# A linear-attention and Fourier-mixing kernel on one core, with its opening stage rebuilt

## The chip, the core and the metric

The kernel runs on 1 core of one Trainium2 chip. The time is device microseconds of one execution, from the launch to the last output, as the median of several runs. Before the change it is 1011.36 us (3 runs, 1010.89 to 1011.57). The five engines of the core work through instruction queues of their own: TensorE (PE in the profile, its weight loads PEld), VectorE (DVE), ScalarE (ACT), GpSimd (POOL) and SyncE (SP). SP here only issues transfers, which run on 16 DMA engines.

## The reference

All of it is float32, with batch 8, 8 heads, 576 tokens, 64 columns to a head, and so 512 columns in all.

```python
def _attn_ref(q, k, v):                      # q, k, v: (8, 8, 576, 64)
    q_s = exp(q - max(q, -1)); q_s = q_s / (sum(q_s, -1) + 1e-9)
    k_s = exp(k - max(k, 2));  k_s = k_s / (sum(k_s, 2) + 1e-9)
    kv = einsum('bhsd,bhse->bhde', k_s, v)
    return einsum('bhsd,bhde->bhse', q_s, kv)

def _moe_ref(x, w_ch1, w_ch2):               # x: (8, 576, 512)
    mixed = real(fft(fft(x, axis=1), axis=2))
    u = x + mixed
    un = (u - mean(u, -1)) / sqrt(var(u, -1) + 1e-6)
    return u + maximum(un @ w_ch1, 0) @ w_ch2  # w: 512 x 2048, 2048 x 512
```

The kernel gets k transposed (columns by tokens), q and v with the heads side by side, and the two weight matrices as pairs of 32-bit words that it has to turn into float32 on the chip. Two tables come from the host: `ft` with cosines and sines over tokens, `cd` over columns.

## The kernel before

The work goes by groups of 512 tokens. Of a batch's 576 tokens, 512 make its own four tiles of 128 x 512; the 64 that are left are gathered from all batches into a ninth group. For each group come attention, folds of tokens and columns (which use the symmetry of the Fourier transform to quarter its products), two stages of products with `ft` and `cd`, a norm, and two layers of products with the weights. The first layer ("plain", lines 1435 to 1475) is computed directly for batch 0, while the weights are converted and combined; all later groups run on combined weights. No loop is on the chip: the program lists every step with a due time, sorts the steps, and so fixes the order of each engine's instructions. An engine never takes a later instruction first; where one waits, all behind it on that engine wait. The due times give an order and no clock.

The opening is written out by hand: the string `OPENING` names each step with its time. Steps `k00` to `k03` are batch 0's keys for pairs of heads (`max`, `exp`, four transposes `turn`, a copy `four`, and the product with the values `kv`); `k0 last` and `k0 fifth` transpose the last 128 tokens. A, B, C and D are batch 0's own tiles of queries and `t` the 128 rows of tokens that are shared with batch 1. They are exponentiated, transposed and multiplied by the key-value products, which stand as full 128 x 128 blocks in `kv0` (zeros off the two heads' blocks); a further product with `ones` gives the sums for the division. Then `tokens`, `columns`, `by` and `again` fold the rows on VectorE, `b0` to `b4` are the blocks of frequencies on TensorE (lines 1196 and 1199), `m0` and `m1` the second transform of the two halves of tokens (lines 1270, 1273), `s` the statistics of the four tiles, `normal`, `turn` and `laid` the normalized, transposed tiles. Among these stand `k10` to `k13`, the keys of batch 1 in the same way as batch 0's, and `c0`, the conversion of the first block of weights. `WARM` adds products whose result nobody reads.

The loads of the opening are issued by SP in the order that `loads_first` gives: keys of batch 0 (4 loads), the first half of the queries, the first half of the values (2), the second half of the queries, the shared tokens (4 loads of 32 rows, line 305), the other half of the values (2), 4 rows that replace rows of the shared tokens (line 308), the tables, keys and values of batch 1 (12), and eleven blocks of raw weights.

The first layer multiplies sixteen blocks of channels, `up(f)`, each of four products of 128 x 512 (line 1441). Block 0 runs as two halves of 256 columns (`half`, line 1450), since the tiles with c = 0 are normalized first. Each block of weights is converted by ACT (lines 409, 410), VectorE (403, 406) and POOL (411). VectorE also forms the combined weights (461) while the layer runs.

Later batches take their keys in another form, `keys(b)`: loads `kb` and `vt` with another layout (lines 676, 688), maxima on VectorE (732), an exchange between partitions, sixteen exponentials on ACT (736), transposes on VectorE (745), and products that use half of TensorE's columns (754).

Of the kernel before, what the change touches and what calls it, by code (L numbers as in the profile page):

```python
# [87 lines left out]
WARM = (3, 3), (24.7, 6), (41.9, 2), (43.45, 1), (44.5, 1)  # L88
# [4 lines left out]
10.80 A exp, 11.20 k00 kv, 11.30 k03 four, 11.84 B exp, 11.85 A turn, 12.20 C max, 12.30 k01 kv, 12.45 A copy,  # L93
12.80 D max, 12.95 B turn, 12.95 C less, 13.40 A ones, 13.55 B copy, 13.99 D less, 14.10 C exp, 14.20 k02 kv,
14.35 A inverse, 14.85 C turn, 15.00 t max, 15.14 D exp, 15.30 k03 kv, 15.75 t less, 15.95 D turn,
16.35 k0 scale0, 16.40 B ones, 16.47 t exp, 16.80 k0 scale1, 17.14 t inverse, 17.25 B kv, 17.99 B inverse,
18.22 A kv, 18.35 C copy, 18.39 t normal, 19.01 B out, 19.19 t turn, 19.32 D copy, 19.63 k10 max, 19.69 C ones,
19.84 t copy, 20.30 A out, 20.43 k10 exp, 20.49 C kv, 20.92 C inverse, 21.39 t fold, 21.46 D ones,
22.26 D kv, 22.40 C out, 22.51 D inverse, 23.53 D out, 23.60 t join, 23.65 k10 turn, 23.70 t kv, 24.15 tokens0,
24.36 t parts, 24.77 tokens1, 25.39 columns0, 25.46 k10 four, 25.75 columns1, 25.80 t rest, 26.23 by1, 26.59 by0,  # L100
26.80 c0 hi, 26.95 t folds, 27.45 c0 lo, 27.60 t rows, 27.70 again0, 28.00 again1, 28.50 tokens3, 28.60 b0 times,
29.12 tokens2, 29.58 b1 times, 29.74 columns3, 29.80 b0 copies, 30.10 columns2, 30.56 b4 times, 30.58 by2,
30.78 b1 copies, 30.94 by3, 31.42 again2, 31.72 again3, 31.76 b4 copies, 32.22 k12 max, 32.32 b2 times,
32.89 c0 shift, 33.02 k12 exp, 33.30 b3 times, 33.59 c0 sign, 33.78 b2 copies, 34.19 k13 max, 34.28 k12 turn,
34.31 c0 add, 34.50 b3 copies, 34.86 k11 max, 35.05 k13 exp, 35.20 m0 times, 35.81 k12 four, 36.10 k13 turn,
36.31 m0 copy, 36.55 m1 times, 36.66 k11 exp, 36.81 m0 sums, 37.42 k13 four, 37.61 k1 last, 37.71 m0 add0,
37.92 m1 copy, 38.07 k11 turn, 38.27 k1 fifth, 38.39 m0 add1, 38.42 m1 sums, 38.77 k11 four, 38.92 k10 kv,
39.22 s00, 39.27 roots, 39.67 k11 kv, 39.69 m1 add1, 39.97 s01, 40.42 k12 kv, 40.87 root0, 40.99 m1 add0,
41.17 k13 kv, 41.67 scales0, 41.87 s11, 42.02 normal01, 42.62 s10, 42.77 turn01, 43.37 normal00, 43.52 root1,
43.87 scales1, 43.89 normal11, 43.95 laid01, 44.02 turn00, 44.22 normal10, 44.77 laid00, 44.87 turn10,  # L110
45.47 turn11, 45.62 laid10, 46.22 laid11, 53.00 k1 inverse, 53.30 k1 scale0, 53.60 k1 scale1"""
# [30 lines left out]
class _Block:  # L142
    def __init__(self, ctx, tc, q, kT, v, w1, w2, ft, cd, out):
# [6 lines left out]
        self.ps = pool("ps", space=bass.MemoryType.PSUM)  # L150
        for n in ("ba", "bb", "bc"):
            self.ps.tile([P, 512], F32, tag=n, name=n)
        self.banks(0)
        ctx.callback(lambda: self.small_banks.__exit__(None, None, None))
# [7 lines left out]
        for b in range(2):  # L162
            t = c.tile([P, NR, DH + 1], F32, name=f"pairs{b}")
            nc.gpsimd.memset(t[:], 1.0)
            self.pairs.append(t)
        t = self.work.tile([P, KT, HD], F32, tag="Z", name="Z", bufs=1)
        self.kv0 = t[:].rearrange("p k n -> p (k n)")[:, 0:NR * P].rearrange("p (r n) -> p r n", r=NR)
        nc.gpsimd.memset(self.kv0, 0.0)

# [19 lines left out]

        self.ones = c.tile([P, NR, H], F32, name="ones")  # L190
        nc.gpsimd.memset(self.ones[:], 0.0)
        for h in range(2):
            nc.gpsimd.memset(self.ones[64 * h:64 * h + 64].rearrange("p r h -> p (r h)")[:, h::H + 2], 1.0)
# [39 lines left out]
    def banks(self, late):  # L233

        if late:
            self.small_banks.__exit__(None, None, None)
        self.late = late
        self.small_banks = self.tc.tile_pool(name=f"banks{late}", bufs=1, space=bass.MemoryType.PSUM)
        self.ps2 = self.small_banks.__enter__()

    def acc(self, shape, two=False):
        if self.late:
            t = self.two()[:, 0, :] if two else self.ps2.tile([P, 512], F32, tag="one", name="one")
        else:
            t = self.ps2.tile([P, 512], F32, tag="acc", name="acc", bufs=3)
        return t[:shape[0], :shape[1]]

    def two(self):
        return self.ps2.tile([P, 2, 512], F32, tag="two", name="two", bufs=2)

    def turned(self):
        if self.late:
# [17 lines left out]
    def warm(self, n):  # L270

        t = self.ps.tile([P, 512], F32, tag="ba", name="ba")
        for _ in range(n):
            self.nc.tensor.matmul(t[:, 0:2 * P], lhsT=self.ident[:], rhs=self.pairs[1][:].rearrange("p r n -> p (r n)")[:, 0:2 * P],
                                  start=True, stop=True)
# [4 lines left out]
    def loads_first(self, fetch):  # L280
# [9 lines left out]
        ks = [place(S) for _ in range(NR)]  # L290
        v = place(NC * D).rearrange("p (c n) -> p c n", n=D)
        own = [place(2 * D).rearrange("p (c n) -> p c n", n=D) for _ in range(2)]
        tail = place(D)

        at = NF * D - NR * (S + NC * P)
        k1, v1 = [place(S) for _ in range(NR)], [place(NC * P) for _ in range(NR)]
        self.second_at = k1, [t.rearrange("p (c n) -> p c n", n=P) for t in v1]
# [3 lines left out]
        def shared():  # L301
            flat = self.q[b:b + 2].rearrange("b s n -> (b s) n")
            for i in range(4):
                a = i * S // 2 + P
                load(tail[i * Q:(i + 1) * Q], flat[a:a + Q])

        def shared_firsts():
            load(tail[0:P:Q], self.q[b:b + 2].rearrange("b s n -> (b s) n")[::S // 2])
# [17 lines left out]
        def second(r):  # L326
            cols = slice(r * P, (r + 1) * P)
            t = self.second_at[1][r]
            load(self.second_at[0][r], self.kT[1, cols, :])
            load(t[:, 0:4, :], self.v[1, 0:512, cols].rearrange("(c p) n -> p c n", p=P))  # L330
            load(t[:, 4, :], self.v[1, S - P:, cols])
# [4 lines left out]
        return [(i / 100, step) for i, step in enumerate(order)]  # L336

# [18 lines left out]
    def tables(self):  # L356
        self.nc.sync.dma_start(self.ft[:], self.ft_dram)
        self.nc.sync.dma_start(self.cd[:], self.cd_dram)

    def weights(self):
# [23 lines left out]
        def convert(i):  # L386
# [5 lines left out]
            n = ("bc", "bb", "bc")[i] if i < 3 else "acc"  # L392
            if i < 26:
                t = self.ps.tile([P, 512], F32, tag=n, name=n)[:] if i < 3 else self.acc((P, D))
            else:

                t = hi.bitcast(F32)
# [114 lines left out]
    def attention_timed(self, b, start, end):  # L512
# [14 lines left out]
        for t, *some in visits:  # L527
            jobs = [self.t_times_kv(b) if it == "t" else self.own_times_kv(it, i == 1) for i, it in enumerate(some)]
# [23 lines left out]
    def first_keys(self, b):  # L552

        nc, V = self.nc, self.nc.vector
        ks, v = self.at_start[:2] if b == 0 else self.second_at
        v = [v[:, :, r * P:(r + 1) * P] for r in range(NR)] if b == 0 else v
        copy, box, top = nc.vector.tensor_copy if b == 0 else nc.scalar.copy, {}, {}
# [33 lines left out]
        def times(r):  # L591
            if r == 0:
                box["kv"] = self.acc((P, D)).rearrange("p (r n) -> p r n", n=P)
            for c in range(NC):
                left = self.kss[r][:, c, :] if c < 4 else self.fifth[:, r, :]
                nc.tensor.matmul(box["kv"][:, r, :], lhsT=left, rhs=v[r][:, c, :], start=c == 0, stop=c == NC - 1)

        def scale(h):
            s = slice(64 * h, 64 * h + 64)
            V.tensor_tensor(out=self.pairs[b][s, :, 0:DH] if b else self.kv0[s, :, s], in0=box["kv"][s, :, s],  # L600
                            in1=rec[s].unsqueeze(2).to_broadcast([64, NR, 64]), op=ALU.mult)
# [6 lines left out]
        for h in range(2):  # L608
            step(f"k{b} scale{h}", scale, h)
        return steps  # L610

    def opening(self, fetch, converted):
# [4 lines left out]
        steps = {**self.first_keys(0), **self.first_keys(1)}  # L617
# [16 lines left out]
        named("t kv,t parts,t folds,t rest,t rows", self.t_times_kv(0))  # L634
        for n, it in own.items():
            named(f"{n} max,{n} less,{n} exp", self.q_exp_spread(it))
            named(f"{n} turn,{n} copy", self.q_turn(it))
            named(f"{n} ones,{n} kv,{n} inverse,{n} out", self.q_times_kv(it))
        for name, f in zip(("tokens", "columns", "by", "again"), self.folded(0)):
            for i in range(4):  # L640
# [1334 lines left out]
```

## Time and profile before

| what | us |
|---|---|
| median of 3 runs, in all | 1011.36 |
| the profiled execution, in all | 1013.53 |
| its span, first to last instruction | 1011.7 |
| TensorE busy in the span | 999.8 |
| VectorE, ScalarE, GpSimd busy | 717.4, 493.9, 443.2 |
| first product of the first layer starts at | 50.78 |
| moved by DMA | 236.18 MB |

The profile takes one execution. Lines such as L1441 are lines of the kernel. "x8" counts records; a float32 product of TensorE leaves two records. A row of the stages ("11.03:27.73 ...") has the length, then each engine's busy time with its number of records, the granted share of TensorE's clock, the mean busy share of the 16 DMA engines, and GB/s. A row of a timeline has start, length, engine, line and operation, output and input, and in brackets the idle time before it and what ended that. A row of the groups by line ends with busy us, mean ns of one, and idle time before. The chain of waits is followed back from the last instruction; its rows have start, length, and what that time went to.

### The profile page before, as it was taken

To read this page: it belongs to the slowest core of one execution; us is meant where nothing else is said; L and a number is where in the kernel's file an instruction comes from. 1 tells how busy PE (TensorE), PEld (TensorE's weight loads), DVE (VectorE), ACT (ScalarE), POOL (GpSimd) and SP (SyncE) were. 2 spreads that over 40 slices of the span, in tenths; PEclk is the share of its full clock that TensorE was granted. 3 is DMA by queue.
4 is the path that set the end of the run, shared out by engine and by line. 5 is a ranking of instruction groups with operands and counts; after the bars stand their busy time and mean duration, and the time that the engine had idled before them with its cause. 6 is when DMAs were issued, how large, how long until landed. Compare 5 with 4: busy or idle time off the path is not lost.

```text
span 1011.7 us, 19333 instructions
## 1 busy us (share of the span) xinstructions
PE 999.8 (99%) x7326; PEld 858.6 (85%) x7326; DVE 717.4 (71%) x1352; ACT 493.9 (49%) x1266; POOL 443.2 (44%) x447
## 2 busy tenths in 40 slices
PE   8999999999999999999999999999999999999998
PEld 7844564888888899889988998899889998998898
DVE  5888897766765787678756887688656935685563
ACT  5584633782368238752776267725782242151210
POOL 4164420347535546565656456664646360040000
PEclk9999999999999999999999999999999999999999
DMA  8878399796999766875768577947654755675563
GB/s 263 268 238 296 125 246 324 232 245 219 309 316 256 227 229 240 234 247 210 277 199 242 209 263 247 255 179 265 227 189 156 270 195 199 225 263 186 182 248 137
DMA packets 122004, 236.18 MB, mean 233 GB/s; under 512 B 24040, under 2 KB 86376, under 8 KB 111288
## 3 DMA queue, kind: packets, MB, share of 16 engines
q1 hardware_dynamic: 121544, 234.43, 70.8%
q8 instruction: 58, 0.95, 0.4%
q14 instruction: 34, 0.28, 0.1%
q10 hardware_dynamic: 288, 0.26, 0.1%
q0 software_dynamic: 80, 0.26, 0.1%
HBM read 199.79 MB, written 39.06 MB: 236 GB/s over the span
## 4 chain that ended last, share of the span: by engine, by line
PE 84%; DVE 8%; DMA 4%; ACT 1%; issue 1%; POOL 1%; SPq 0%; ACTq 0%; DVEq 0%; POOLq 0%
PE bb L1525 15%; PE ba L1525 10%; PE bb L1652 10%; PE bc L1525 10%; PE ba L1652 7%; PE bc L1652 7%; PE bb L1622 5%; PE bb L1441 2%; PE ba L1441 2%; PE bc L1441 2%; PE one L754 2%; PE two L1232 1%; DMA big<-w1s 1%; PE bb L1741 1%; PE ba L1741 1%; PE two L1270 1%
## 5 line engine op out<-in xcount | busy, mean ns | idle before, releaser
L1525 PE MATMUL bb<-unT,big 128*128 128x256 f32 x768 | 183.3, 380 | 0.4 <-DVE u L1495 0.4
L1525 PEld LDWEIGHTS bb<-unT,big 128*128 128x128 f32 x768 | 144.7, 190 | 21.6 <-DVE u L1495 1.1
L1537 ACT ACTIVATE big<-big 128x512 f32<-128x512 f32 x96 | 59.8, 629 | 147.1 <-DVE big L1536 140.3
L1525 PE MATMUL ba<-unT,big 128*128 128x256 f32 x512 | 123.9, 382 | 1.4 <-DMA big<-w1s 1.3
L1525 PE MATMUL bc<-unT,big 128*128 128x256 f32 x512 | 121.5, 380 | 0.1
L816 ACT ACTIVATE qT<-q 32x128 f32<-32x128 f32 x384 | 117.9, 307 | 5.9 <-DVE q L806 0.7
L1525 PEld LDWEIGHTS bc<-unT,big 128*128 128x128 f32 x512 | 96.9, 190 | 13.7 <-DVE big L1536 0.5
L1525 PEld LDWEIGHTS ba<-unT,big 128*128 128x128 f32 x512 | 95.5, 190 | 15.2 <-DMA big<-w1s 1.5
L1495 DVE TENSOR_TENSOR u<-bb,s 128x512 f32<-128x512 f32 x66 | 45.2, 684 | 84.5 <-PE bb L1525 66.5
L1652 PE MATMUL bb<-big 128*128 128x128 f32 x848 | 103.8, 276 | 0.2 <-DVE u L1659 0.2
L1652 PEld LDWEIGHTS bb<-big 128*128 128x128 f32 x848 | 98.9, 192 | 1.0 <-DVE u L1659 1.0
L1375 POOL COPY unT<-unT 32x256 f32<-32x256 f32 x98 | 42.3, 432 | 91.4 <-DVE unT L1367 87.2
L1602 POOL TENSOR_TENSOR x<-x,big 128x512 f32<-128x512 f32 x45 | 61.0, 1369 | 46.0 <-DVE big L1659 19.7
L1598 DVE TENSOR_TENSOR big<-big 128x512 f32<-128x512 f32 x98 | 79.8, 842 | 0.0
L1652 PE MATMUL ba<-big 128*128 128x128 f32 x640 | 79.0, 276 | 0.0
L1652 PEld LDWEIGHTS ba<-big 128*128 128x128 f32 x640 | 75.0, 192 | 0.8
L1375 ACT COPY unT<-unT 32x256 f32<-32x256 f32 x126 | 50.7, 402 | 32.0 <-DVE unT L1367 30.2
L803 POOL TENSOR_TENSOR q<-q,qm 128x512 f32<-128x512 f32 x24 | 25.8, 1073 | 91.3 <-DVE qm L798 65.9
L417 POOL TENSOR_TENSOR big<-big 128x512 f32<-128x512 f32 x24 | 30.4, 1268 | 67.4 <-ACT big L1537 67.4
L1622 PE MATMUL bb<-big 128*128 128x256 f32 x256 | 58.3, 379 | 0.0
L1536 DVE TENSOR_TENSOR big<-bc,u 128x512 f32<-128x512 f32 x64 | 44.0, 687 | 16.5 <-PE bc L1525 15.7
L1622 PEld LDWEIGHTS bb<-big 128*128 128x128 f32 x256 | 48.0, 190 | 6.1
(320 smaller groups left out, 1925.6 us busy)
## 6 DMA issues: line engine op xcount, KB each, us to landing
big<-w2d SPq DMA_DIRECT2D x67, 1024.0 KB, 4.6
big<-w1s SPq DMA_DIRECT2D x64, 896.0 KB, 4.6
big<-w2s SPq DMA_DIRECT2D x16, 1024.0 KB, 4.8
big<-in_w_dram SPq DMA_DIRECT2D x21, 512.0 KB, 5.5
w2d<-big SPq DMA_DIRECT2D x42, 256.0 KB, 6.8
kb<-in_kT_dram SPq DMA_DIRECT2D x24, 320.0 KB, 7.2
q<-in_q_dram SPq DMA_DIRECT2D x28, 256.0 KB, 6.0
vt<-in_v_dram SPq DMA_DIRECT2D x72, 80.0 KB, 5.0
```

The lines of the kernel that those rows point to most:

```text
L417: e1.tensor_tensor(out=to(4), in0=at(2), in1=at(3), op=ALU.add)
L816: nc.scalar.activation(to[t, i * Q:i * Q + Q], one, ACT.Exp)
L1375: copy(to, of)
L1441: nc.tensor.matmul(ph[:], lhsT=self.w1sb[:, f, k * P:(k + 1) * P], rhs=unT()[:, k // 2 * 2:k // 2 * 2 + 2, k % 2, :], start=(k == 0), stop ...
L1495: plus = lambda t: V.tensor_tensor(out=temp(t), in0=box["bb"][:], in1=box["s1"][:], op=ALU.add)
L1525: nc.tensor.matmul(bank()[:, i, :], lhsT=w[:, WA_AT[m], k * P:(k + 1) * P], rhs=self.unT[g][:, B_AT[m], k, :], start=first and i == 0 and ...
L1536: steps = [(0, lambda: V.tensor_tensor(out=hp(i), in0=bank()[:], in1=u()[:], op=ALU.add)), (0.8, lambda: nc.scalar.activation(hp(i), hp(i) ...
L1537: (0.8, lambda: nc.scalar.activation(hp(i), hp(i), ACT.Relu))]
L1598: e.tensor_tensor(out=to(o), in0=to(x), in1=to(y), op=op)
L1602: E.tensor_tensor(out=x, in0=x, in1=tile(m), op=ALU.add)
L1622: nc.tensor.matmul(box[name][:, i, :], lhsT=h[p][:, A_AT[m], i * P:(i + 1) * P], rhs=self.stream[n][:, p, :], start=p == 0 and (m != 1 or ...
L1652: nc.tensor.matmul(box[place[n]][:, i, :], lhsT=own(m)(A_AT[n])[:, f, :], rhs=w[:, r // 2, r % 2 * P:r % 2 * P + P], start=first and f == ...
```

## The change

The attention of batch 0 uses the form of the later batches: keys and values are multiplied in halves of 64 columns straight into the layout `pairs0` with a column of ones, and queries in tiles of 64 x 64 (`by_head`), so that the sums come with the product; `kv0` and `ones` go. PSUM is divided in three phases in place of two. The loads are issued in another order: both halves of the queries, then the shared tokens as four loads of 31 rows, then the values; the four single rows go first, on ACT's queue; keys and values of batch 1 come behind the weights, in the layout of `keys(b)`. For the cosine part the fold by frequency is left to TensorE (`early`): each of two token folds is multiplied twice, once with a negated table `less`. Tile C is divided on ACT, and the shared tokens' fold runs wholly on POOL. The tile of `m0` is added to a copy of x in PSUM (`kept`), the tiles with c = 0 are normalized and transposed first, and the first three blocks of channels run in halves; the mean and the spread of the last tile are taken on ACT. Two more blocks of weights are converted in the opening. The keys of batch 1 become `keys(1)` inside the first layer.

```diff
-WARM = (3, 3), (24.7, 6), (41.9, 2), (43.45, 1), (44.5, 1)
+WARM = (2, 4, 256), (7.26, 1, 64), (8.52, 1, 64), (18.63, 2, 256), (22.111, 10, 256)
+BY_ACT, BY_DVE = "C", (2, 3)
+KEYS_AT = (0, 6, 14, 14.3, 16, 24.3, 26), (13, 20, 32, 35, 36, 43, 44)
...
@@ loads_first
-                load(tail[i * Q:(i + 1) * Q], flat[a:a + Q])
+                load(tail[i * Q + 1:(i + 1) * Q], flat[a + 1:a + Q])
         def shared_firsts():
-            load(tail[0:P:Q], self.q[b:b + 2].rearrange("b s n -> (b s) n")[::S // 2])
+            nc.scalar.dma_start(tail[0:P:Q], self.q[b:b + 2].rearrange("b s n -> (b s) n")[::S // 2])
...
-        order = [lambda: nc.gpsimd.memset(v[0:64, 4, :], 0.0), table, *(lambda r=r: keys(r) for r in range(NR)), lambda: queries(0),
-                 lambda: values(0), lambda: queries(1), shared, lambda: values(2), shared_firsts, self.tables,
-                 *(lambda r=r: second(r) for r in range(NR)), *(lambda i=i: fetch(i) for i in range(11))]
+        order = [shared_firsts, lambda: nc.gpsimd.memset(v[0:64, 4, :], 0.0), table, *each(keys), lambda: queries(0), lambda: queries(1),
+                 shared, lambda: values(0), lambda: values(2), self.tables, *(lambda i=i: fetch(i) for i in range(11))]
+        later = [step for _, step in self.keys_to(1) + [(0, self.prepare)] + self.values_to(1, 0)]
...
@@ first_keys
-                nc.tensor.matmul(box["kv"][:, r, :], lhsT=left, rhs=v[r][:, c, :], start=c == 0, stop=c == NC - 1)
+                for h in range(2):
+                    s = slice(64 * h, 64 * h + 64)
+                    nc.tensor.matmul(box["kv"][s, r, 0:DH], lhsT=left[:, s], rhs=v[r][:, c, s], start=c == 0, stop=c == NC - 1)
...
@@ own_times_kv
+                if act:
+                    for h in range(2):
+                        for n in range(r.start, r.stop):
+                            nc.scalar.activation(x[:, h, n, :], px[:, h, n - r.start, 0:DH], ACT.Copy, scale=rec[:, h, n:n + 1])
+                    continue
...
@@ blocks
+        def early(c):
+            t, first = eo[c], opened(0)
+            for k, back in ((0, 0), (0, 1), (1, 0), (1, 1), (4, 0)):
+                a = QD if k == KT else HD * back
+                for odd in (1, 0):
+                    minus = (c and odd) != (back and k)
+                    f = (1 - odd) * MO
+                    nc.tensor.matmul(bank(k, odd), lhsT=t[:, a:a + P], rhs=(self.less if minus else self.ft)[:, f:f + ME - odd],
+                                     start=first and k == 0 and not back, stop=False, skip_group_check=True)
...
@@ norm
+        def mean(i):
+            uns[i] = self.halves()
+            nc.scalar.activation(uns[i][:, 0:D], self.xpart(g, i % 2, i // 2), ACT.Copy, scale=1.0 / D, accum_out=mv[:, i, 0:1])
...
+        def spread(i):
+            nc.scalar.activation(uns[i][:, 0:D], self.xpart(g, i % 2, i // 2), ACT.Square, bias=box.pop(i)[:, 0:1], scale=D ** -0.5,
+                                 accum_out=mv[:, i, 1:2])
...
@@ plain
-        first[0] = [(-0.9, lambda: half(0)), (0, lambda: half(1)), (2.5, lambda: relu(0))]
+        for f, dt in ((0, 6), (1, 4.5), (2, 2.7)):
+            first[f] = [(dt, lambda f=f: relu(f))]
...
-    steps.append((first + 60, blk.prepare))
+    steps += [(first + np.interp(dt, *KEYS_AT), step) for dt, step in blk.keys(1, 0)]
```

The string `OPENING` is written anew. Its order in the changed program, from the values on: `k00 kv`, `k01 kv`, turn of C, `k02 kv`, `k03 kv`, turn of D, product of A, turn of `t`, products of C, B and D, product of `t`, the two `early` folds, the sine products, the tails, `m0`, `m1`, ten products of `WARM`, turns of the two tiles with c = 0, the halves of blocks 0 and 1, the other two turns, and four more halves.

More of the change, by code (lines that the diff above doesn't have):

```diff
@@ L97 @@
[L97 to L111, printed above, removed]
+10.80 A exp, 11.30 k03 four, 11.84 B exp, 11.85 A turn, 12.20 C max, 12.45 A copy,
@@ L1257, in copies, with second @@
             nc.scalar.copy(paired(zt[:, w + Q:w + W]), both(even + NT - 1, odd + NT - 2, NT - 1, -1))
-        return own, tails, copies
-    def second(self, z, zr, adds, two=True):
+        return own, tails, copies, early, sine
+    def second(self, z, zr, adds, two=True, apart=None):
         nc, V = self.nc, self.nc.vector
```

389 lines of the change are left out of this document (197 added, 192 removed).

## The prediction

> **What bounds the kernel now.** I read the page, then who waited for whom on TensorE, then the busy time of each engine by stage, then the chain of waits up to the first layer.
>
> ```profile
> span 1011.7 us, 19333 instructions
> PE 999.8 (99%) x7326; PEld 858.6 (85%) x7326; DVE 717.4 (71%) x1352; ACT 493.9 (49%) x1266; POOL 443.2 (44%) x447
> ...
> PE ba L274 <- POOL pairs L164: 1.9, 1, 1.9
> PE tr L574 <- ACT big L569: 1.7, 2, 1.2
> ...
> PE tr L1350 <- ACT unT L1359: 0.5, 1, 0.5
> PE bb L1525 <- DVE u L1495: 0.4, 2, 0.2
> ```
>
> TensorE is busy 99% of the span, and its waits (us in total, times, longest) are small, the largest two 1.9 and 1.7 us and both before 9 us. So work taken off another engine is worth something only where TensorE runs behind that engine, and TensorE work that is added to a full stage costs all of its time. The stages, with their borders taken from the chain below:
>
> ```profile
> core 0: us, PE busy (x) PEld busy (x) DVE busy (x) ACT busy (x) POOL busy (x), PEclk, DMA share, GB/s
> 0.00:11.03 11.03, 6.93 (x27) 4.66 (x27) 4.85 (x7) 6.29 (x14) 6.76 (x25) 0.98 0.84 254
> 11.03:27.73 16.70, 16.13 (x128) 15.73 (x128) 11.27 (x30) 6.92 (x13) 4.50 (x6) 0.91 0.93 275
> 27.73:50.78 23.05, 22.40 (x158) 20.02 (x159) 20.32 (x54) 15.09 (x40) 4.37 (x5) 1.00 0.81 262
> 50.78:61.73 10.95, 10.76 (x35) 6.17 (x34) 9.24 (x17) 9.34 (x17) 5.75 (x5) 1.00 0.46 141
> 61.73:114.53 52.80, 52.80 (x239) 24.51 (x239) 46.93 (x77) 32.45 (x60) 26.50 (x21) 1.00 0.79 275
> ```
>
> ```profile
> 3.08 7.91 DMA big<-in_v_dram
> ...
> 11.03 2.50 PE acc L596 x10
> ...
> 18.29 1.12 PE acc L596 x10
> 19.41 0.44 PE tr L965 x4
> ...
> 27.81 1.20 DVE eo L1140 x2
> ...
> 61.73 3.43 PE ba L1441 x8
> ```
>
> The chain has three parts. Until 11.03 us everything waits for the first half of batch 0's values; then TensorE carries the attention; from 27.7 us VectorE carries the token folds, frequency blocks and norm until TensorE starts the first layer at 50.78 us (27.73 is where the first fold starts on VectorE's timeline). From there TensorE is full: in 61.73 to 114.53 it is busy 52.80 of 52.80 us, while VectorE is busy 46.93, so idle only 5.87. I measure the change at the product of the fourth block of channels, 61.73 us, the first that has one form in both kernels, and add what the first layer itself gains or loses after it.
>
> **The change part by part.** First the loads. On SP's queue the order was keys, one half of the queries, the first half of the values; now it is keys, both halves of the queries, then four loads of the shared tokens, each of 31 rows of 2 KB, and only then both halves of the values. The four-row load that waited behind the shared rows goes to ACT's queue; this takes away SP's wait below, 2.9 us.
>
> ```profile
> SPq L308 <- DMA big<-in_q_dram: 2.9, 1, 2.9
> ...
> out_dram<-xs SPq DMA_DIRECT2D x16, 32.0 KB, 3.2
> out_dram<-xs SPq DMA_DIRECT2D x16, 30.0 KB, 4.2
> ...
> 80.00:90.00 10.00, 10.00 (x25) 4.48 (x24) 6.79 (x12) 4.27 (x9) 3.94 (x3) 1.00 1.01 376
> ...
> 13.36 1.28 DVE L948 TENSOR_REDUCE qm<-big 128x8 f32<-128x512 f32 x2 [1.41 <-DMA big<-in_q_dram]
> ```
>
> No load here has 31 rows. Its cost has two ends. Spread over all 16 engines, the four (0.25 MB) take 0.7 us at 376 GB/s. On a single engine, a sixteenth of 376 is 23.5 GB/s, so 63.5 KB take 2.7 us and the four 10.8 us, and that engine's share of every later load queues behind them. The nearest rows are the output stores of 16 rows (32 KB, 3.2 us to landing) and of 15 rows (30 KB, 4.2 us): fewer bytes, later. The ragged count leans to the far end, so I take 10.8 us, the largest choice in this sum. The Trainium skill speaks against this edit as well: "DMA: Bandwidth & Descriptors", section "Why a DMA increments its semaphore by 16 and not by 1", says that a copy issued from SP runs on the largest number of engines up to 16 that divides the slowest dimension of both sides; 31 is prime, so one engine would carry each load. At that page's 27 GiB/s for an engine the four would take 8.8 us as an estimate, and the sum would be 2 us lower; no run so far shows a load of 31 rows.
>
> Keys and queries are 2.23 MB, as many bytes as lay ahead of 11.03 us before, so they land near 10.7. Then 10.8 us for the shared rows and 1.4 us for that engine's 32 KB share of the first values: the values land at 22.9 us, not 11.0. What waits: VectorE's maximum of the shared rows, now ahead of the subtraction for tile D, and on TensorE all products of keys and values, since only two turns of queries stand before them. Without the 10.8 the values would land at 14.1: 13.36, where the second queries landed before with as many bytes ahead, plus 0.7.
>
> Second, attention from the values to the first fold.
>
> ```profile
> 188.04 1.32 PE one L754 x40
> ...
> 107.86 0.62 PE acc L832 x32
> ...
> L1044 DVE TENSOR_TENSOR x<-acc,qrec 128x512 f32<-128x512 f32 x4 | 2.7, 682 | 0.6 <-PE acc L1030 0.6
> ...
> L1036 DVE RECIPROCAL qrec<-qrec 128x8 f32<-128x8 f32 x4 | 0.8, 203 | 0.1
> ...
> L1035 DVE TENSOR_SCALAR qrec<-bb 128x8 f32<-128x8 f32 x2 | 0.3, 167 | 2.1 <-PE bb L1019 2.0
> ...
> 7.25:10.66 3.41, 1.85 (x12) 1.29 (x12) 2.55 (x5) 2.58 (x6) 0.72 (x1) 1.00 1.07 351
> 10.66:14.07 3.41, 3.23 (x16) 3.04 (x15) 1.93 (x5) 1.63 (x3) 1.32 (x2) 0.50 1.05 231
> ```
>
> Products in halves of the array already exist: 20 of the key-value kind take 1.32 us (two records each), 16 of the by-head kind 0.62. Keys and values in this form are 40 products, 2.6 us, before 20 full ones (4 x 1.12 in the chain); a turn 0.44; the scaling 0.42 (128 x 256 on VectorE, as the sums below); tile A's product 0.62; then VectorE's drain of A, B and D (0.37 for sum and inverse, 0.68 for the product) and C's inverse, 3.5, while ACT scales C: 7.6, with handovers 8.0. After a sparse window (1.85 of 3.41 us busy) the granted clock was 0.50 for 3.41 us; here TensorE would idle some 9 us before the values, so I add 1.3 us (most of the 1.7 that a window at half clock loses; bounds 0 and two windows, 3.4). Tokens0 starts at 22.9 + 9.3 = 32.2, not 27.7: of the 11.9 us lost, 7.4 come back (9.3 in place of 16.70).
>
> Third, from the first fold to the first layer. By the order of instructions VectorE loses two frequency folds and two column folds, all of batch 1's key maxima and two of the four per-tile statistics ahead of the first half, and gains two early conversions of weights and two copies.
>
> ```profile
> L1140 DVE TENSOR_TENSOR eo<-x 128x512 f32<-128x512 f32 x4 | 2.6, 684 | 0.0
> ...
> L1160 DVE TENSOR_TENSOR eo<-eo 128x128 f32<-128x128 f32 x4 | 1.2, 294 | 0.1
> ...
> L1153 DVE TENSOR_TENSOR eo<-eo 128x257 f32<-128x257 f32 x4 | 1.5, 422 | 0.1
> ...
> L1287 DVE TENSOR_TENSOR eo<-acc,sn 128x256 f32<-128x256 f32 x4 | 1.5, 416 | 1.0 <-ACT sn L1279 1.0
> ...
> L1320 DVE BATCH_NORM_STATS2 st<-x 128x6 f32<-128x512 f32 x4 | 2.7, 671 | 0.0
> ...
> L1341 DVE TENSOR_SCALAR eo<-x,std,mv 128x512 f32<-128x512 f32 x2 | 1.1, 532 | 0.0
> ...
> L406 DVE SCALAR_TENSOR_TENSOR big<-bc,big 128x512 int32<-128x512 int32 x1 | 0.7, 692 | 0.0
> ```
>
> VectorE's work up to the first two normalized tiles: token folds 2.5, the first two column folds in four pieces of 0.29, 1.2, shared rows 1.05, the other columns and frequencies 1.5, columns again 1.1, two conversions 2.75, two copies 0.8, two sums 1.8, one addition 0.8, two statistics 1.6, scales and normals 1.2: 16.3. TensorE's added folds (20 products of 145 columns, 4.9 us) run under it; the sine products and tails do not, nor the root on ACT: 1.4 us. A turn and a copy: 1.6. So 19.3 us, before 23.05.
>
> Fourth, the first three blocks of channels in six halves: 10.85 us of products, as before, plus two pairs of turns that now stand between them (0.9) and 0.9 us until the second two tiles are normalized: 12.6, before 10.95. Sum: 22.9 + 9.3 + 19.3 + 12.6 = 64.1, against 61.73: 2.4 us later.
>
> Fifth, batch 1's keys in the layer. On TensorE 40 products, 2.6 us, nothing hides them. On VectorE:
>
> ```profile
> L732 DVE TENSOR_REDUCE km<-kb x24: 807/808/814, 176.9 to 710.4; 128x4 f32<-128x640 f32 x24
> ...
> L745 DVE STREAM_TRANSPOSE kb<-kb x18: 823/842/846, 185.3 to 720.2; 128x640 f32<-128x640 f32 x18
> ...
> L764 DVE TENSOR_TENSOR pairs<-one,krec x12: 290/292/293, 191.6 to 732.5; 128x128 f32<-128x128 f32 x12
> ```
>
> four maxima (3.2), four transposes (3.4), two exchanges and two scalings (1.9), 8.5, less 1.2 for the old scaling that goes: 7.3 net against 5.87 idle in that stage. I take the overflow, 1.4 us, as a stall later, because the 0.5 and 0.4 us waits on TensorE's list show VectorE arriving just late at the next layer. Bounds: 0 and 7.3. On ACT sixteen exponentials lie in a stage where it is busy 32.45 of 52.80 us: nothing. Their twelve loads stand on SP behind the eleven weight loads and ahead of the reloads of freed weight places, whose conversions they would hold up if they came late; the eight for the second value half stand among the weight writes. The four fills for them on POOL stand ahead of its fold, in a wait: nothing. The fill moved to VectorE lies under its wait for the first keys.
>
> Total: 2.4 + 2.6 + 1.4 = 6.4 us. The profiled execution took 1013.5 us in all, its span 1011.7 and 1.8 around it; the runs shown have a median of 1011.36 in all, 2.2 less. I put the sum on the median: 1017.8.
>
> **The rivals.** (1) Faster: the 31-row loads spread like any other. For it: all rows of loads with 32, 64 and 128 rows. Against: the 15-row stores. Values at 14.1, tokens0 at 22.5 (no clock loss, 0.4 for the second value half), the fourth block at 54.4, 7.3 earlier: 1011.4 - 7.3 + 2.6 + 1.4 = 1008.1. (2) VectorE becomes the bound of the first layer: nothing of the 7.3 us is absorbed, as conversions wait in order behind maxima whose loads are late. It decides once the work added to VectorE passes the 5.87 us that are idle. 1017.8 + 5.9 = 1023.7. Against: 5.87 idle there. (3) No change: the loads run on two engines, 5.4 us in place of 10.8, and the clock stays full: 57.4 for the fourth block, 4.3 earlier, and 1011.4 - 4.3 + 2.6 + 1.4 = 1011.1. For and against it stand the rows of rival 1.
>
> **How the numbers follow.** Forecast 0.58 with its own range 1014 to 1021.5 (0 or 3.4 for the clock, 0 or 4 for VectorE's stall, 9.7 to 10.8 for the loads); rival 1 0.24; rival 2 0.09; rival 3 0.09. Within 0.2% (2.0 us, about what a measurement here can tell) lies rival 3 and the edge of rival 1. Faster 0.25, same 0.10, slower 0.65. The range reaches to rival 1 and leaves out rival 2: 1006.5 to 1022.
>
> **What would show it.** Right: key-value products wait on the load of values until past 20 us at a DMA share near 0.1 of the sixteen engines, half clock after; the first fold near 32; the fourth block near 64; 40 more key-value records twice in the layer. Wrong: values landing before 16 us, the fourth block before 58, or VectorE idle less than 1 us in the layer with TensorE waiting for converted weights.

## The result, and the profile after

The changed kernel takes 1017.29 us (median of 6 runs, 1015.53 to 1019.20) beside 1011.15 us for the kernel before on the same chip (6 runs, 1010.03 to 1013.09): a ratio of 1.0059, 95% interval 1.0044 to 1.0075. The forecast was 1017.8, within 1006.5 to 1022.0. The profiled execution took 1019.2 us in all, its span is 1017.4; like the one of before (1013.53) it lies 2 us above its median, so the two profiles can be set side by side.

The head of the page after:

```profile
span 1017.4 us, 19783 instructions
...
PE 994.0 (98%) x7546; PEld 853.8 (84%) x7546; DVE 718.5 (71%) x1355; ACT 495.3 (49%) x1285; POOL 442.1 (43%) x445
```

Who waited for whom on TensorE (us in total, times, longest):

```profile
PE two L585 <- DMA big<-in_v_dram: 7.8, 1, 7.8
PE ba L1543 <- DMA big<-w1s: 2.7, 1, 2.7
...
PE bc L1456 <- ACT big L1471: 0.5, 1, 0.5
```

TensorE is busy 5.8 us less than before, and yet the span is 5.7 us longer: one wait for the values, 7.8 us, is longer than all of TensorE's idle time of before up to the first layer (5.3, from the stage rows in the prediction). The stages after, cut at the steps where the prediction cut them (values, first fold, first product of the first layer, fourth block of channels), and at the second layer:

```profile
0.00:21.13 21.13, 9.51 (x41) 6.35 (x41) 8.14 (x14) 9.73 (x19) 8.43 (x25) 0.79 0.68 219
21.13:31.61 10.48, 9.86 (x224) 8.40 (x224) 6.48 (x19) 4.74 (x13) 2.40 (x7) 0.77 0.99 310
31.61:50.35 18.74, 16.25 (x164) 14.47 (x165) 16.88 (x45) 10.42 (x31) 5.77 (x8) 1.00 1.04 245
50.35:61.66 11.31, 11.31 (x56) 10.03 (x57) 9.61 (x18) 8.26 (x16) 5.63 (x5) 1.00 0.55 188
61.66:112.38 50.72, 50.22 (x270) 23.68 (x268) 46.17 (x83) 34.25 (x75) 22.73 (x18) 1.00 0.80 266
```

The last of these stages in the kernel before, up to its second layer:

```profile
61.57:108.41 46.84, 46.84 (x189) 21.34 (x188) 41.14 (x68) 28.50 (x52) 24.20 (x20) 1.00 0.80 277
```

| stage | before | forecast | after |
|---|---|---|---|
| values have landed | 11.03 | 22.9 | 21.13 |
| values to first fold | 16.70 | 9.3 | 10.48 |
| first fold to first layer | 23.05 | 19.3 | 18.74 |
| halves, to the fourth block | 10.79 | 12.6 | 11.31 |
| fourth block starts | 61.57 | 64.1 | 61.66 |
| fourth block to second layer | 46.84 | 46.8 + 4.0 | 50.72 |

All starts here are from TensorE's and VectorE's timelines. The prediction has 61.73 for the fourth block before, from the chain, which lets a product begin only where the one ahead of it ends; on the timeline it starts at 61.57.

The 10.1 us that the late values cost are given back by shorter attention (6.2) and folds (4.3): at the fourth block the two kernels are level. Nearly all that is lost lies behind it: 3.9 us in the first layer, and later 1.4 us more in one wait for combined weights (`w1s`: 2.7 us; before 1.3, by the row below). TensorE's wait before:

```profile
PE ba L1525 <- DMA big<-w1s: 1.3, 1, 1.3
```

### The profile page after: what moved, and what is told of

The parts are those of the page before. It is cut to its first block, busy times and chain, and to the rows that moved or that the text cites. A ratio compares the mean times of both kernels' runs of the same rounds, so it can differ in the third digit from the quotient of the medians.

```text
span 1017.4 us, 19783 instructions
## 1 busy us (share of the span) xinstructions
PE 994.0 (98%) x7546; PEld 853.8 (84%) x7546; DVE 718.5 (71%) x1355; ACT 495.3 (49%) x1285; POOL 442.1 (43%) x445
## 4 chain that ended last, share of the span: by engine, by line
PE 85%; DVE 7%; DMA 4%; issue 1%; SPq 1%; POOL 1%; ACT 1%; DVEq 0%; POOLq 0%
PE bb L1543 15%; PE ba L1543 10%; PE bc L1543 10%; PE bb L1670 10%; PE ba L1670 7%; PE bc L1670 7%; PE bb L1640 5%; PE bc L1478 2%; PE two L839 2%; DMA big<-w1s 2%; PE one L754 2%; PE two L1206 1%; PE two L1263 1%; PE bb L1759 1%; PE ba L1478 1%; PE ba L1759 1%
## 5 line engine op out<-in xcount | busy, mean ns | idle before, releaser
L1620 POOL TENSOR_TENSOR x<-x,big 128x512 f32<-128x512 f32 x45 | 61.0, 1368 | 46.0 <-DVE big L1677 19.7
```

Source lines behind the costliest of these rows:

```text
L1620: E.tensor_tensor(out=x, in0=x, in1=tile(m), op=ALU.add)
```

## The experiments

Twelve kernels. All start from the changed kernel, except `before31`, which starts from the kernel before. A ratio is always to the kernel before, run beside them, with its 95% interval; the last two columns are from one profiled execution each.

| run | us | ratio | first fold | fourth block |
|---|---|---|---|---|
| changed kernel | 1017.29 | 1.0059 (1.0044 to 1.0075) | 31.6 | 61.7 |
| `split` | 1011.1 | 0.9995 (0.9982 to 1.0008) | 24.9 | 54.4 |
| `split29` | 1016.32 | 1.0047 (1.0031 to 1.0063) | 30.7 | 60.7 |
| `before31` | 1021.26 | 1.0098 (1.0084 to 1.0113) | 36.2 | 70.0 |
| `order` | 1019.79 | 1.0073 (1.0053 to 1.0093) | 33.2 | 62.7 |
| `fill` | 1015.86 | 1.0037 (1.0023 to 1.0051) | 29.0 | 60.0 |
| `nokeys` | 1011.63 | 0.9995 (0.9985 to 1.0005) | 31.3 | 60.9 |
| `splitorder` | 1011.1 | 0.9996 (0.9986 to 1.0005) | 24.9 | 54.4 |
| `all3` | 1011.62 | 0.9998 (0.9983 to 1.0013) | 24.6 | 54.6 |
| `rows32` | 1012.92 | 1.0014 (1.0003 to 1.0024) | 27.6 | 57.1 |
| `swapd` | 1012.04 | 1.0003 (0.9991 to 1.0015) | 25.3 | 54.9 |
| `rows32d` | 1012.78 | 1.0009 (0.9999 to 1.0018) | 26.6 | 56.1 |
| `tlate` | 1015.34 | 1.0038 (1.0024 to 1.0052) | 23.5 | 57.0 |

### Is it the 31 rows?

`split`:

```diff
-                load(tail[i * Q + 1:(i + 1) * Q], flat[a + 1:a + Q])
+                for m, n in ((1, Q // 2), (Q // 2, Q)):
+                    load(tail[i * Q + m:i * Q + n], flat[a + m:a + n])
```

> Each of the four loads of 31 rows is made in two, of 15 and 16 rows; all else as in the changed kernel. Theory (a load of 31 rows runs on one DMA engine, so the four hold one engine for some 10 us and that engine's share of the values comes last): the longest wait of TensorE for the load of values, 7.8 us in the changed kernel, falls under 2 us, the key-value products start near 14 us in place of 21.1, half clock ends early, and the time falls by about 7 us, from 1017.3 to near 1010. Rival (31 rows are spread over the engines like others, and the values are late because the sixteen engines serve the tables and weights issued behind them at the same time): no change within 1 us, the wait stays near 7.8.

The key-value products start at 14.35 us, the mean clock of the profiled execution is 0.999 (0.993 in the changed kernel), and the median is 6.2 us lower. TensorE's wait for the values:

```profile
PE two L586 <- DMA big<-in_v_dram: 2.0, 2, 1.6
```

The fourth block comes at 54.4, the very time that the prediction worked out for its first rival, though not by the way it worked it out (the first fold is at 24.9, not 22.5). But the gain alone would also be there if eight small loads were simply better than four.

`split29` cuts the same loads at `Q - 2` in place of `Q // 2`: 29 and 2 rows.

> Each of the four loads of 31 rows is made in two, as in the run with 15 and 16 rows, but of 29 and 2 rows: again eight loads, the same bytes. Theory (the row count decides on how many engines a load runs, and 29, a prime, still means one): issuing the eight takes SP as long as the four took (5 us) or longer, the busy share of the sixteen engines falls to 0.1 to 0.3 between 8 and 12 us, TensorE waits 6 to 8 us for the values, and the time stays at 1016 to 1018. Rival (what helped was the larger number of smaller loads): like the run with 15 and 16 rows, the key-value products from 14.4 us on, 1011.

`before31` puts the ragged count into the kernel before, where these loads stand behind the first half of the values:

```diff
-                load(tail[i * Q:(i + 1) * Q], flat[a:a + Q])
+                load(tail[i * Q + 1:(i + 1) * Q], flat[a + 1:a + Q])
```

> The kernel before with one edit: its four loads of 32 rows become 31 rows (the first row of each comes with the four-row load in any case, and SP's wait ahead of that load goes with it). Theory (the ragged row count alone costs it): SP's queue is held behind these loads, the second half of the values comes at about 17 to 20 us in place of 14, the third key-value product of batch 0 and the attention behind it wait 3 to 6 us, and the time rises by 2 to 6 us, to 1013.5 to 1017. Rival (31 rows cost nothing by themselves; only their place ahead of the values does): within 1 us of 1011.4.

The stretch from 10 to 12 us of `split29` (length, the busy time of the engines, clock, busy share of the sixteen DMA engines, GB/s):

```profile
10.00:12.00 2.00, 1.50 (x9) 1.13 (x8) 1.90 (x5) 1.29 (x3) 1.68 (x2) 0.64 0.07 27
```

Its wait for the values, and the longest wait of `before31`:

```profile
PE two L586 <- DMA big<-in_v_dram: 7.1, 1, 7.1
```

```profile
PE acc L596 <- DMA big<-in_v_dram: 7.3, 1, 7.3
```

SP's issues of the second half of the values in `before31` (start, length):

```profile
9.30 2.47 SPq L319 DMA_DIRECT2D big<-in_v_dram  x1
11.81 2.59 SPq L320 DMA_DIRECT2D big<-in_v_dram  x1
```

Eight loads with 29 rows among them are as slow as four of 31; a share of 0.07 is one engine of sixteen (0.0625). And in the kernel before, where nothing else was touched, one row less makes it 9.4 us slower (1021.26 beside 1011.82): more than the 2 to 6 expected, because the third group of key-value products then waits 7.3 us and the clock falls to half behind it (0.50 at 18 to 24 us). The edit also starts each load one row later; but `split` and `split29` both do that, and only `split29` is slow. The count of rows is the cause. The Trainium skill's rule ("DMA: Bandwidth & Descriptors", section "Why a DMA increments its semaphore by 16 and not by 1"), a copy from SP takes the largest number of engines up to 16 that divides the slowest dimension, agrees with the counts tried here: 31 and 29 slow, 32, and 15 with 16, not.

### How one engine holds up the others

`order` leaves the loads of 31 rows and issues the values ahead of them:

```diff
-                 shared, lambda: values(0), lambda: values(2), self.tables,
+                 lambda: values(0), lambda: values(2), shared, self.tables,
```

> The two halves of the values are issued ahead of the four loads of 31 rows, which stay as they are. Theory (one engine is held by the four loads, and whatever is issued behind them has its share on it late): TensorE's wait for the values falls under 2 us and the key-value products start near 14 us, but the maximum of the shared rows on VectorE stays near 20 us or later and holds tile D behind it, and the tables, next in the queue, come no earlier; the total lies between, 1011 to 1016. Rival (the sixteen engines serve all open loads at once, and the share of each sinks with their number): the values are as late as before, within 2 us, and the total within 1 us of 1017.3.

The values are there when they are needed (products from 13.9 us, no wait). But the total is no better: its median is 2.5 us above the changed kernel's, outside what the theory gave, though the intervals of the two ratios overlap. The maximum of the shared rows on VectorE's timeline (in brackets the idle time ahead of it):

```profile
22.70 0.69 DVE L967 TENSOR_REDUCE qm<-big 128x8 f32<-128x512 f32 x1 [9.83 <-DMA big<-in_q_dram]
```

TensorE's wait that it ends in:

```profile
PE tr L984 <- ACT big L976: 7.5, 1, 7.5
```

Behind that maximum stand, in order, the subtraction for tile D, its exponential and TensorE's turn of D. The delay was moved onto another path, not taken away. SP's queue (start, length) shows how the ragged loads reach the others. Here are the issues of the first half of the values in the changed kernel:

```profile
8.63 2.41 SPq L309 DMA_DIRECT2D big<-in_v_dram  x1
11.08 2.46 SPq L310 DMA_DIRECT2D big<-in_v_dram  x1
```

The same two in `order`, ahead of the ragged loads:

```profile
3.61 0.47 SPq L309 DMA_DIRECT2D big<-in_v_dram  x1
4.12 0.58 SPq L310 DMA_DIRECT2D big<-in_v_dram  x1
```

An issue that takes 0.47 us takes 2.41 behind the ragged loads. This reads as SP standing still until the one engine has room, while the other fifteen run dry; no view shows the engine's queue itself. The changed kernel's DMA share by time:

```profile
10.00:12.00 2.00, 0.55 (x6) 0.42 (x4) 1.90 (x4) 1.46 (x3) 1.51 (x2) 1.00 0.17 47
12.00:14.00 2.00, 1.26 (x6) 0.66 (x4) 0.78 (x2) 1.38 (x4) 1.67 (x5) 0.59 0.73 250
...
18.00:20.00 2.00, 0.00 (x0) 0.00 (x0) 0.00 (x0) 0.00 (x0) 0.00 (x0) 0.50 0.89 321
```

The share at 10 to 12 us does not by itself mark a ragged load: in `split` it is 0.23 there, since SP needs 6.8 us for its eight issues. The packets do. All that moved from 10 to 11 us in the changed kernel:

```profile
DMA packets 13, 0.03 MB, mean 27 GB/s; under 512 B 0, under 2 KB 0, under 8 KB 13
q1 hardware_dynamic: 13, 0.03, 6.8%
```

These are rows of 2 KB, one by one, 0.08 us apart. The trace's list of packets has them so from 9.3 to 19.26 us: 124 rows, the four ragged loads, on one engine. From 12 us on the other engines go ahead with the values, the tables and the weights. The values are 1152 packets of 1 KB; 1080 of them, 15 of every 16, have started by 17.73 us, and the next one only at 19.26, as the last ragged row ends. From there the missing sixteenth comes one by one, and TensorE starts at 21.13. `split29` shows the same: 1080 packets, then none until its last 2 KB row ends at 18.42.

### What the half clock costs

`fill` adds one entry to `WARM`:

```diff
+WARM = ..., (13.99, 18, 256), ...
```

> Eighteen more products of 256 columns, whose result nobody reads, stand ahead of the first key-value product, in the time in which TensorE waits for the values; the loads stay as in the changed kernel. Theory (the half clock from 12.3 to 26.0 us comes from TensorE's idle time and costs the products of keys and values and the turns after 21.1 us some 2.6 us): the granted clock is 1.00 from 21 us on and the first fold comes 2 to 3 us earlier, the time 1014.5 to 1015.5. Rival (the first fold is held by VectorE and by the loads, not by TensorE's clock): the clock is full and the first fold and the time stay within 0.7 us, 1017.3.

In the changed kernel the granted clock is 0.50 in one stretch:

```profile
12.34:26.00 13.66, 5.82 (x76) 4.97 (x78) 3.39 (x7) 3.47 (x6) 1.63 (x5) 0.50 0.83 262
26.00:28.00 2.00, 2.00 (x57) 1.68 (x54) 1.18 (x3) 0.59 (x1) 0.00 (x0) 1.00 1.06 309
```

In `fill` it is 1.00 there:

```profile
22.00:24.00 2.00, 2.00 (x49) 1.75 (x46) 1.06 (x3) 1.00 (x2) 0.00 (x0) 1.00 1.05 343
```

and the first fold on VectorE's timeline, at 31.61 in the changed kernel, comes 2.6 us earlier:

```profile
29.04 1.20 DVE L1103 TENSOR_TENSOR eo<-x 128x512 f32<-128x512 f32 x1
```

Of the 2.6 us, 0.4 come from values that landed at 20.7 in this execution; 2.1 are the clock (8.3 us from the values to the first fold, in place of 10.48). At the fourth block 1.7 are left, in the median 1.4, where the intervals of the two ratios overlap: the stretch from the first fold to the first half grew from 18.7 to 19.7 us; what took it was not looked into.

### What the keys in the first layer cost

`nokeys` keeps only the last four steps of `blk.keys(1, 0)`, the loads of values, and leaves out batch 1's keys.

> Leaves out batch 1's keys in the first layer: their maxima, exponentials, transposes and products (the loads of the values stay), so batch 1's output has stale key-value products. Theory (only TensorE's 40 products count, the rest lies beside it): 2.6 us faster, 1014.7, with the block of channels after the opening still at 61.7 us. Rival A (VectorE's and ScalarE's added work stalls the layer by 1.4 us besides, as predicted): 4.0 us faster, 1013.3. Rival B (VectorE becomes the bound of the layer): 6 us or more faster, under 1011.3.

The whole difference is 5.7 us, between two of the expected values, but it does not all belong to the keys. The stage from the fourth block to the second layer is 46.84 us here (60.85 to 107.69), as long as in the kernel before, and 50.72 in the changed kernel. So the keys cost the layer 3.9 us, all that it lost, close to the 4.0 of rival A. The rest lies elsewhere: in this execution the fourth block came 0.8 us earlier, and TensorE did not wait for `w1s` at all. In the groups of the stage by line (busy us, mean ns of one, idle time before), changed kernel:

```profile
L1456 PE MATMUL bc<-unT,big 128*128 128x512 f32 x32 | 14.6, 598 | 0.5 <-ACT big L1471 0.5
L1456 PE MATMUL bb<-unT,big 128*128 128x512 f32 x32 | 14.5, 596 | 0.0
L754 PE MATMUL acc<-vt,kb 128*64 128x65 f32 x60 | 2.1, 223 | 0.0
L754 PE MATMUL acc<-vt,Z 128*64 128x65 f32 x20 | 0.8, 227 | 0.0
```

without the keys:

```profile
L1456 PE MATMUL bc<-unT,big 128*128 128x512 f32 x32 | 14.4, 592 | 0.0
```

So of the 3.9 us that the layer lost, the key products are 2.9, slower block products 0.3 (592 ns without the keys, 4 to 6 more with them, on 64 records), and one wait 0.5; 0.2 is spread over the rest. That wait is not for VectorE. ScalarE's timeline ahead of it:

```profile
76.59 1.28 ACT L736 ACT_TABLE_LOAD   x1
77.88 0.43 ACT L736 ACTIVATE kb<-kb,km 128x160 f32<-128x160 f32 x1
78.22 0.66 ACT L397 ACTIVATE big<-big 128x512 int32<-128x512 uint32 x1
78.77 0.58 ACT L1471 ACTIVATE big<-bc 128x512 f32<-128x512 f32 x1
```

The relu (the maximum with 0) of the bank that TensorE wants next stands behind the loading of the exponential's table. `all3` (both changes of the loads, and `KEYS_AT` with 23.5, 34, 37, 38, 45, 46 in place of 20, 32, 35, 36, 43, 44) moves the exponentials back:

> As the run with both changes of the loads, and in the first layer the exponentials of batch 1's keys (with the loading of their table on ScalarE, 1.28 us) come some 3 us later, spread closer. Theory (0.5 us of the layer's loss is one relu that stands on ScalarE behind that table load): TensorE's wait for ScalarE in the layer, 0.5 us, goes, and the layer from the fourth block to the second layer is 50.2 us in place of 50.7 to 51.5. Rival (the relus are only moved into another collision): the wait comes back under another block, the layer stays at 50.7 to 51.5.

The rival was right, and the layer is longer than it said: 52.4 us (54.6 to 107.0). The same 0.5 us comes back under another block, whose relu again stands behind the table load and two exponentials, and VectorE is 1.1 us late with a division ahead of a turn. TensorE's longest waits in the layer:

```profile
PE tr L985 <- DVE q L957: 1.1, 1, 1.1
PE ba L1457 <- ACT big L1472: 0.5, 1, 0.5
```

### Can the opening come earlier still?

`splitorder` is `split` and `order` together.

> The loads of 15 and 16 rows, and the two halves of the values issued ahead of them. Theory (with eight small loads ahead SP still reaches the values only at 10.4 us, and the engines run dry at 10 to 12 us, share 0.23): the values come 1.5 to 2.5 us earlier, TensorE's 2.0 us of waits for them go, the shared rows come before they are needed, the first fold comes 0.5 to 2 us earlier than the 24.9 of the run with 15 and 16 rows, the time 1009 to 1010.5. Rival (from 13 us on ScalarE's exponentials and the turns set the attention, not the values): the key-value products begin no earlier than 13.9 us and the fold within 0.4 us of 24.9, the time 1011.

The products start at 12.5 us, 1.9 earlier than in `split`, and the first fold is where it was, 24.9. TensorE now waits for VectorE's scaling of the key-value products (line 589, 1.6 us), which stands behind the shared rows' chain. Three runs went after that chain: four loads of 32 rows behind the values, with the four-row load on SP behind the tables (`rows32`), "D less" ahead of "t max" (`swapd`), and both (`rows32d`).

> The changed kernel with the shared tokens in four loads of 32 rows, as in the kernel before, but behind the values, and with the four-row load back on SP, behind the tables. Theory (after the ragged loads are gone the next limit is that eight small loads hold SP until 13.7 us and bring the shared rows late; four loads do not): SP reaches the tables by 10 to 12 us, the busy share at 12 to 14 us is over 0.6 in place of 0.26, and the first fold comes 0.5 to 1.5 us earlier than 24.9, the time 1009.5 to 1010.5. Rival (the four-row load waits for the 32-row ones and comes as late as the eight loads did): the maximum of the shared rows stays at 15 us or later, the fold within 0.4 us of 24.9, the time 1011.

> The values ahead of the loads of 15 and 16 rows, and on VectorE the subtraction of tile D ahead of the maximum of the shared rows. Theory (tile D's exponential and turn, TensorE's wait of 1.5 us, stand behind VectorE's wait for the shared rows): TensorE's 2.5 us of waits for ScalarE shrink to 1 us or less and the first fold comes 0.5 to 1.5 us before 24.9, the time 1010 or less. Rival (the shared rows' own chain, maximum, exponential, turn, product, sets the first fold): the fold within 0.4 us of 24.9, the time 1011.

> Both of the two runs above together: four loads of 32 rows behind the values, and tile D ahead of the shared rows on VectorE. Theory: the first fold at 23 to 24 us, the fourth block at 52.5 to 53.5, the time 1009 to 1010, below both kernels. Rival (from the first fold on VectorE and ScalarE set the opening, or the gain is lost in the layer): the fourth block within 0.5 us of 54.4, the time 1011.

None helped. In `rows32` the four-row load, which must wait for the other rows, lands so late that VectorE stands still for 4.91 us; in `swapd` and `rows32d` TensorE's wait for the scaling grows to 3.0 and 4.0 us, since the scaling was left behind the shared rows. VectorE's timeline of `rows32`:

```profile
17.75 0.69 DVE L967 TENSOR_REDUCE qm<-big 128x8 f32<-128x512 f32 x1 [4.91 <-DMA big<-in_q_dram]
```

The last run moves the scaling, tile D and the division of tile A ahead of what waits for the shared rows:

```diff
-... 13.00 t max, 13.10 D less, 13.20 t less, ... 14.13 t exp, ... 14.75 t inverse, 14.76 k0 scale, 14.8 t normal, 15.0 A kv, 15.1 t turn,
+... 13.00 D less, ... 14.31 k0 scale, 14.32 t max, 14.33 t less, ... 14.45 t exp, 15.0 A kv, ... 15.5 A inverse, 15.51 A out,
+18.60 C inverse, 18.61 C out, 18.615 t inverse, 18.616 t normal, 18.62 D kv, 18.64 t turn, 18.65 t copy, ...
```

> The values ahead of the loads of 15 and 16 rows, and on VectorE the scaling of batch 0's key-value products, tile D and the division of tile A ahead of what waits for the shared rows; the shared rows' turn on TensorE behind the products of all four tiles. Theory (in the last four runs VectorE stood 2 to 5 us before the maximum of the shared rows, and the scaling behind it, 0.42 us, held TensorE 1.6 to 4.0 us): TensorE's wait for the scaling falls under 0.5 us, the first fold comes at 22 to 23.5 us in place of 24.9, the fourth block at 52 to 53.5 in place of 54.4, the time 1008.5 to 1010, below both kernels. Rival (the shared rows' late products then hold the folds by frequency on TensorE instead): the first fold is early, but the fourth block stays within 0.5 us of 54.4, the time 1011.

TensorE's longest wait in it:

```profile
PE two L840 <- POOL F L1026: 4.9, 1, 4.9
```

The first fold comes at 23.5, the earliest of all, and the fourth block at 57.0: what the fold gained, TensorE loses in front of the products of the shared rows, whose fold on GpSimd now comes late. The rival named the place; its time was too good. But the execution profiled is the fastest of nine (1011.93; the others reach 1019.92), and what makes the median 3.4 us longer these rows don't show; it was not looked into. No run here is below both kernels by more than its interval: `split` and `splitorder` remove the loss of the change and end level with the kernel before.

## Why the prediction was right, and where it was not

The sign came out, and the two largest causes, the ragged loads and the keys, were the ones named. That the total came out to 0.5 us is luck in part. The opening was 2.4 us better than forecast, the layer cost about what was forecast, though not by the mechanism that was given, and a wait that the sum did not have (1.4 us) filled most of the gap.

1. The ragged loads: right, on one engine. The cause is shown by `split`, `split29` and `before31`. The size was 1.8 us too large: the values landed at 21.13, not 22.9. The engine began with the ragged rows at 9.3, not 10.7; it took 9.9 us for them, not 10.8 (26 GB/s while it was alone, not 23.5); and its part of the values took 1.9, not 1.4. What they cost, read against `split`, is 6.8 us at the first key-value product and 7.3 us at the fourth block.
2. What they hold up: half right. "That engine's share of every later load" was late, as foretold. But the prediction expected a DMA share near 0.1 until past 20 us; that lasted 2 us. It left out that SP itself is held (0.47 us of issue becomes 2.41), and that once it is free the other fifteen engines run ahead.
3. The clock: the direction right, the 1.3 us taken for it too small. `fill` shows 2.1 at the first fold, still within the bounds 0 to 3.4. This is most of why attention took 10.48 and not 9.3.
4. Folds and norm: 18.74 beside 19.3. The halves: 11.31 beside 12.6. TensorE is busy for all 11.31 us of that stage: the turns between the halves take the 0.9 us that was counted for them, but the 0.9 us of waiting for the second two tiles does not come, and the products take 10.4, not 10.85. So the opening gained 1.8 us on the forecast in the loads, 0.6 in the folds and 1.3 in the halves, and lost 1.2 in attention: level with the kernel before, where +2.4 stood in the sum.
5. The keys: 4.0 us expected, 3.9 measured, and all of it undone by `nokeys`. The products alone are 2.9 in place of 2.6. The stall of 1.4 us put down to VectorE's overflow was the wrong mechanism: VectorE worked 46.17 of 50.72 us there and TensorE never waited for it. Of the two waits that the prediction took as a sign of VectorE being late, the one of 0.5 us is for ScalarE by its own row (`unT`, line 1359). What was missed is ScalarE, costed at "nothing" because it had idle time. One wait of 0.5 us is for it; that the table load of 1.28 us ahead of the relu causes it is read from the order on ScalarE in two runs, and no run takes the table load away.
6. Not in the sum: the wait for `w1s`, 1.4 us more than before. It came out between nothing (`nokeys`) and 2.7 us in the profiled executions, and was 1.4 in `split`; whether the change has any part in it stays open.

The prediction's inner range does not follow from its own bounds: 3.4 us for the clock and 4 for the stall add 4.7 to 1017.8, which is 1022.5 and not 1021.5. The result lies well inside either.

Rival 1 was wrong in its condition: the loads are not spread. With spread loads the fourth block does come at its 54.4, but by two errors that cancel: in `split` the first fold is 2.4 us later than it said (24.9, not 22.5), and the stretch from there 2.4 us shorter (29.5, not 31.9). Its total, 1008.1, was 3 us too good: in `split` the layer takes 51.5 us (54.4 to 105.9), 4.7 more than before, so only 2.5 of the 7.1 us gained reach the second layer, and the medians show 0.4 of them, with an interval from 1.8 faster to 0.8 slower. Rival 2 fell: 3.9 us lost in the layer in place of 9.9. Rival 3 fell with the single engine. So the rebuilt opening is worth some 7 us, the keys in the layer take 4 to 5 of them back, and the ragged loads took the rest and more.

## What to carry to other kernels

Look at the row counts of the loads in a change before anything else: `before31` pays 9.4 us for one row less in four small loads, and the price shows in the loads issued behind them, not in these. When a transfer is moved forward to shorten a wait, ask which instruction stands in order behind the one that now waits; seven of these twelve runs only moved a wait to another place. And work moved out of a stage that is not full into one where TensorE is 100% busy cost more than its TensorE time here (3.9 us for 2.9 us of products), though the other engines had idle time.

## What was not expected of the hardware

SP's issue of a load is not free of the loads ahead of it: 2.41 us in place of 0.47 behind the ragged loads. In the kernel before, an issue of queries takes 1.32 us too, in place of 0.43, but at a DMA share of 0.94; behind the ragged loads SP is held at 0.17. An engine that is held back doesn't stop the other fifteen: the share is back at 0.89 at 18 to 20 us, while TensorE waits for the rest of an earlier load. The half clock outlasts its cause: TensorE was busy again from 21.13 us, 2.00 of 2.00 us from 22 on, and the clock came back only at 26.0, 4.9 us later; a lag shows in `all3` too, where it is 0.50 at 12 to 14 us with TensorE busy 2.00 of 2.00 us, after a sparse stretch (0.67 of 2.00 us). The Trainium skill ("TensorE: Matmul & The Clock Gate", Part 1) states that full clock returns after a busy window of about 3.4 us on a free-running grid, which fits a lag between one and two windows.
